# Attention, top-1 MoE and soft MoE in one kernel: seven weight chunks are issued ahead of four others

## The chip, the cores and the metric

One NeuronCore of a Trainium2 chip runs the whole program. The metric is the device time of one execution in microseconds (us); lower is better. All inputs and outputs are float32.

## What is computed

Three layers follow each other: causal attention with a cumulative bias, a mixture of experts that sends each token to one of 8 experts, and a soft mixture of experts with 32 slots. The work around the change is the end of the second layer and the whole of the third.

```python
# x: 2304 tokens x 512 from the attention
for e in range(8):                                # layer 2: one expert per token
    xe = x[expert_idx == e]
    out[expert_idx == e] = gate_w[...] * (np.maximum(xe @ w1[e], 0) @ w2[e])
# layer 3: soft MoE, phi: 512 x 32
logits = x @ phi
d = softmax(logits, axis=0)                       # over tokens
slot_input = (d.T @ x).reshape(8, 4, 512)
for e in range(8):
    slot_out[e] = np.maximum(slot_input[e] @ w1[e], 0) @ w2[e]
c = softmax(logits, axis=1)                       # over the 32 slots
return c @ slot_out.reshape(32, 512)
```

## The kernel before, in words

**Stages.** The attention runs first. From 241.6 us of the span on, layer 2 goes through the experts one by one: `step_unit` (line 1020 multiplies) makes the hidden rows, and the eight functions of `post_units` fold the expert's tokens into the 32 slot inputs `SI`. The last of them, `p4` (line 1160), multiplies with the four `w2` chunks of the expert. For the last expert there is no later expert beside which this could run, so its `post` functions stand alone, in the loop at line 1318, with filler products (`warm`) on TensorE between them. Layer 3 comes last: `f1` (line 1386) multiplies the slot inputs with 32 chunks, `f3` (line 1425) the hidden rows with 32 more, in three blocks of output columns (`COLS`: 256, 128 and 128 wide), and `finish` makes and writes the output of a block (lines 1456 to 1458).

**Chunks and slots.** All weights of layers 2 and 3 come in chunks of 128 partitions x 1024 float32 (512 KB), numbered in the order in which they are used. `M1` is 96: chunks 0 to 95 belong to layer 2 (`ORD`), 96 to 159 to layer 3. The last four of layer 2, 92 to 95, are the `w2` chunks of the last expert. Of layer 3, 96 to 127 are `m1` (used by `f1`), 128 to 143 `m2` and 144 to 159 `m3` (used by `f3`). A chunk gets its place in SBUF from `slot`, which counts the places handed out: a ring of `RING` = 34 slots in three pools (`NFIFO`), so that chunk i + 34 goes where chunk i was. When layer 2's products are done, seven more places appear: the tile `x3`, where the transposed tokens `xT` were (three chunks), and the pool `fifo_d`, where the pool `weights` (split weights and gathered tokens) was (`NLATE` = 4 chunks). `slot` has a number, `first`, from which on the seven are handed out; after these the ring goes on.

**What sets the order.** `fill(n)` issues the DMA of every chunk up to n - 1 that has not been issued, in order of number, on the SP queue. `refill(i)` stands behind the last use of chunk i and lets `fill` go as far as the slot of i allows. Instructions of an engine run in program order, and so does the SP queue: a DMA that waits for its slot holds back every DMA behind it. Line 1317 issues the seven extra chunks. Chunk 126 is the one that takes the slot of chunk 92, the first `w2` chunk of the last expert, and `fill` counts straight on, so all of 126 to 136 are asked for at line 1317, ahead of `post` in the program text. The output is written by DMAs of the SP queue too (line 1458), behind the last chunk. In layer 3, five slots of the ring serve other tiles (`extra`, positions in `EXTRA`), among them the three `c` tiles, which POOL loads from DRAM (line 1349) after its scatters into it (line 1187).

Of the kernel before, what the change touches and what calls it, by code (L numbers as in the profile page):

```python
# [38 lines left out]
NLATE = 4  # L39
RING = sum(NFIFO)  # L40
# [9 lines left out]
M1 = len(ORD)  # L50
# [5 lines left out]
EXTRA = {2: 0, 3: 2, 4: 3, 5: 4, 8: 1}  # L56
# [25 lines left out]
def kernel(ctx, tc, qk, vm, vt, s, wg, w1, w2, phi, m1, m2, m3, out, dbg=None):  # L82
# [52 lines left out]
    def chunk_src(i):  # L135
        if i < M1:
            kind, e, c = ORD[i]
            w, c = (w1 if kind == "w1" else w2), c + 4 * (kind == "wt")
            return w[bass.ds(place[e], 1), c].rearrange("o p n -> (o p) n") if e else w[0, c]
        i -= M1  # L140
        if i < 32:
            return m1[i // 8 * 2 + i % 2, i % 8 // 2]
        if i < 48:
            return m2[(i - 32) // 2, i % 2]
        return m3[(i - 48) // 8, i % 8]

    slot_n = [0]

    def slot(shape, dtype, name):

        i, first = slot_n[0], M1 + RING
        slot_n[0] += 1
        if first <= i < first + 3:
            return x3[0][:, i - first]
        if i >= first + 3:
            k = (i - first - 3) % (NLATE + RING)
            if k < NLATE:
                return fifo[3].tile(shape, dtype, tag="c3", name=name)
            i = k - NLATE + first

        a, b, c = NFIFO
        r = (i - a - b) % RING
        k = int(i >= a) if i < a + b else 0 if r < a else 2 if r < a + c else 1
        return fifo[k].tile(shape, dtype, tag=f"c{k}", name=name)

    def fill(upto, eng=None):
        while len(chunk_t) < min(upto, M1 + 64):
            i = len(chunk_t)
            chunk_t[i] = slot([128, 1024], F32, f"chunk{i}")
            (eng or nc.sync).dma_start(out=chunk_t[i], in_=chunk_src(i))  # L170
# [5 lines left out]
    def refill(i):  # L176
        if i == 0 or len(fifo) < 3 or not place or not full:
            return
        fill(i + 1 + RING + (NLATE + 3 - sum(x <= i - M1 for x in EXTRA) if i >= M1 else 0))

# [706 lines left out]
    def prep(n, ov=False, lo_later=None):  # L889
        if n >= E * 8 or (n in wh_t and not ov):  # L890
            return
        e, j = divmod(n, 8)
        i = CID["w1", e, j // 2]
        raw = half(i, j % 2, ov)
        hi, lo = (wpool[0].tile([128, 512], F32R, tag="xg" if ov else "w" + t, name=f"w{t}{n}", bufs=3)
                  for t in ("hi", "lo"))
        nc.scalar.copy(hi, raw)  # L897
        def low(eng):
            eng.tensor_tensor(out=lo, in0=raw, in1=hi.bitcast(F32), op=ALU.subtract)  # L899

        if lo_later is None:
            low(nc.vector)
        else:
            lo_later.append(low)
        wh_t[-1 if ov else n] = (hi, lo)
        if not ov and j % 2:
            refill(i)
# [145 lines left out]
    def p_unit(e, ov=False):  # L1053
        def f():
            pt = ps.tile([128, 256], F32, tag="y1", name=f"pt{e}", bufs=1)
            for k in range(4):
                i = CID["wt", e, k]
                w = [half(i, h, ov) for h in range(2)]
                for g in range(4):
                    nc.tensor.matmul(pt[32 * g:32 * g + 32, :], lhsT=phi_sb[:, k, :], rhs=w[g // 2][:, 256 * (g % 2):256 * (g % 2) + 256],  # L1060
                                     start=(k == 0), stop=(k == 3), skip_group_check=True)
                if not ov:
                    refill(i)
            P_t[0] = mp.tile([128, 256], F32, tag="P", name=f"P{e}", bufs=1)
            nc.vector.transpose(P_t[0], pt)
        return f
# [23 lines left out]
    def post_units(e, idx, final=False, ov=False):  # L1090
# [64 lines left out]
        def p4():  # L1155
            al, G = d["al"], d["G"]
            si = ps.tile([128, DM], F32, tag="y2", name=f"si{e}", bufs=1)
            for j in range(8):
                g = 32 * (j % 4)
                nc.tensor.matmul(si[g:g + 32, :], lhsT=G[:, 32 * j:32 * j + 32], rhs=half(CID["w2", e, j // 2], j % 2, ov),  # L1160
                                 start=(j < 4), stop=(j >= 4), skip_group_check=True)
                if j % 2 and not ov:
                    refill(CID["w2", e, j // 2])
            for x in (slice(0, 256), slice(256, 512)) if final else (slice(0, 512),):
                nc.vector.scalar_tensor_tensor(out=SI[:, x], in0=SI[:, x], scalar=al[:, 0:1], in1=si[:, x],
                                               op0=ALU.mult, op1=ALU.add)
# [89 lines left out]
    with tc.manual_schedule():  # L1256
# [57 lines left out]
        late.close()  # L1314
        lp = ctx.enter_context(tc.tile_pool(name="fifo_d", bufs=NLATE))
        fifo.append(lp)
        fill(M1 + RING + 3 + NLATE)
        for i, x in enumerate(("p1", "p2", "pg0", "pg1", "pg2", "p4", "p4b", "pc", "pc2")):
            post[x]()
            if i in WARM:  # L1320
# [2 lines left out]
        for j in range(2):  # L1323
            sps = ps.tile([128, 2, 32], F32, tag="tp", name=f"sps{j}", bufs=2)
            for k in range(2):
                x = 256 * j + 128 * k
# [12 lines left out]
        def extra(i):  # L1339

            if i < 2:
                hz_t[i] = slot([128, 4, 8, 32], F32, f"hz{i}")
                nc.gpsimd.memset(hz_t[i], 0.0)
            else:
                t = slot([128, 960], F32, f"c{i}")
                c = t[:, 0:768].rearrange("p (t r s) -> p t r s", t=6, r=4)
                cl = t[:, 768:960]
                for x, d in zip((cl, t[:, 0:192], t[:, 192:384]), c_d):
                    nc.gpsimd.dma_start(out=x, in_=d.rearrange("(p t) s -> p (t s)", t=18)[:, 192 * i - 384:192 * i - 192])
                c_t[i - 2] = c, cl, t  # L1350
# [185 lines left out]
```

## Time and profile before

| | us |
|---|---|
| device time, median of 3 runs | 512.91 (512.44 to 514.46) |
| device time of the profiled execution | 517.06 |
| its span, from first to last instruction | 515.2 |
| TensorE busy | 477.4 (93%) |
| TensorE weight loads busy | 337.6 (66%) |
| VectorE busy | 313.7 (61%) |
| ScalarE busy | 250.6 (49%) |
| GpSimd busy | 183.7 (36%) |
| DMA queue of SP, share of 16 engines | 67.0% |

The profiled execution is one run of its own, 4.15 us above the median; 1.86 us of its time lie outside the span. All times below count from the start of its span. The shares are means over stages with different limits: layer 3 begins at 454.7 us and is about a ninth of the span. Matmuls are pipelined, so a busy TensorE need not be at its peak.

### The profile page before, as it was taken

How to read it: one execution, taken by the hardware profiler on the slowest of the kernel's cores; microseconds unless marked ns; L12 is line 12 of the kernel's file. 1: busy time of each engine (PE TensorE's matmuls, PEld its weight loads, DVE VectorE, ACT ScalarE, POOL GpSimd, SP SyncE). 2: the span in 40 equal slices, each digit the busy share in tenths (PEclk: the TensorE clock that was granted, in tenths of full speed). 3: DMA queues.
4: the chain of work that ended last, by engine and by line, in shares of the span. 5: the costliest groups of instructions: out<-in, count | busy, mean ns of one | idle time of the engine just before them, and what ended most of it. 6: DMA issues, size and time to landing. Idle time of an engine off the chain costs nothing.

```text
span 515.2 us, 11829 instructions
## 1 busy us (share of the span) xinstructions
PE 477.4 (93%) x4313; PEld 337.6 (66%) x4318; DVE 313.7 (61%) x910; ACT 250.6 (49%) x700; POOL 183.7 (36%) x248
## 2 busy tenths in 40 slices
PE   7888899999999999998979999999999999999876
PEld 2466666677677676677858777777777777434445
DVE  6586768977897798454743746565657566222322
ACT  4466877767767776741323434344344434111202
POOL 6234430953294335160143333333324031236000
PEclk9789999999999999999998999999999999999985
DMA  3755665376646542313699999994996967599998
GB/s 113 257 174 178 197 217 180 80 244 203 213 140 221 184 145 93 112 40 101 239 384 405 408 405 408 406 337 125 396 405 209 377 236 295 202 352 391 408 401 278
DMA packets 45171, 130.87 MB, mean 254 GB/s; under 512 B 6191, under 2 KB 14705, under 8 KB 43184
## 3 DMA queue, kind: packets, MB, share of 16 engines
q1 hardware_dynamic: 42016, 123.34, 67.0%
q0 software_dynamic: 2896, 6.66, 3.8%
q8 instruction: 36, 0.59, 0.5%
q14 instruction: 31, 0.25, 0.1%
q10 hardware_dynamic: 192, 0.01, 0.0%
HBM read 114.78 MB, written 11.13 MB: 244 GB/s over the span
## 4 chain that ended last, share of the span: by engine, by line
PE 35%; DMA 9%; DVE 3%; issue 2%; ACT 2%; POOL 0%; POOLq 0%; DVEq 0%; SPq 0%; ACTq 0%
PE h L1020 17%; DMA chunk<-in_m_dram 7%; PE gt L1140 3%; PE pt L1060 2%; PE si L1160 2%; PE op L1456 2%; PE xTp L1011 2%; DMA xg<-xg_d,sidxu 1%; PE lg L1077 1%; DMA chunk<-in_w_dram 1%; PE hp L1386 1%; PE gt L1150 1%; PE acc L1425 1%; PE warm L249 1%; PE lr L1107 1%
## 5 line engine op out<-in xcount | busy, mean ns | idle before, releaser
L1020 PE MATMUL h<-xT,whi 128*128 128x304 f32 (+5 forms) x512 | 114.2, 314 | 1.5 <-ACTq L1197 1.5
L1020 PEld LDWEIGHTS h<-xT,whi 128*128 128x128 f32 x512 | 84.1, 190 | 15.6 <-issue 11.7
L1020 PE MATMUL h<-xT,wlo 128*128 128x256 f32 (+5 forms) x256 | 77.6, 303 | 0.0
L494 ACT COPY aT<-tp 128x512 f32<-128x512 f32 (+3 forms) x128 | 55.4, 452 | 43.4 <-PE tp L487 31.1
L428 DVE CUSTOM_DVE_ANT_0 sa<-sc,mask 128x384 f32<-128x384 f32 (+3 forms) x128 | 60.6, 484 | 23.9 <-PE sc L425 21.7
L438 ACT ACTIVATE sa<-sa,mx 128x128 f32<-128x128 f32 (+3 forms) x128 | 71.2, 561 | 2.1 <-DVE mx L428 1.7
L1048 ACT ACTIVATE hb<-h 128x304 f32<-128x304 f32 (+5 forms) x64 | 26.9, 420 | 73.6 <-PE h L1020 61.5
L541 PE MATMUL oTp<-aT,v 128*64 128x320 f32 (+4 forms) x448 | 59.5, 374 | 0.0
L487 PE MATMUL tp<-ident,sa 128*128 128x128 f32 x320 | 53.8, 285 | 2.2 <-ACT sa L438 2.1
L899 DVE TENSOR_TENSOR wlo<-chunk,whi 128x512 fp32r<-128x512 f32 x61 | 41.7, 683 | 22.6 <-ACT whi L897 22.2
L425 PE MATMUL sc<-ks,qs 128*128 128x384 f32 (+3 forms) x128 | 51.7, 406 | 2.8 <-DVE mx L428 2.5
L390 POOL TENSOR_TENSOR ks<-qk,ks 64x576 fp32r<-64x576 f32 x31 | 45.4, 1479 | 16.1 <-ACT ks L370 12.2
L425 PE MATMUL sc<-kb,qs 128*128 128x384 f32 (+3 forms) x128 | 42.6, 332 | 7.3 <-DMA kb<-trs 2.8
L487 PEld LDWEIGHTS tp<-ident,sa 128*128 128x128 f32 x320 | 35.4, 143 | 21.1 <-issue 11.4
L1187 POOL DMA_INDIRECT c_d<-L,idxm x22 | 22.9, 1041 | 73.4 <-DVE wlo L899 59.0
L1020 PEld LDWEIGHTS h<-xT,wlo 128*128 128x128 f32 x256 | 48.6, 190 | 0.0
L370 POOL CAST ks<-qk 128x1152 fp32r<-128x1152 f32 x13 | 14.9, 1149 | 72.8 <-PE sc L452 67.7
L897 ACT CAST whi<-chunk 128x512 fp32r<-128x512 f32 x64 | 39.0, 612 | 0.2 <-DVE ch L712 0.2
L541 PEld LDWEIGHTS oTp<-aT,v 128*64 128x64 f32 (+1 forms) x448 | 24.0, 135 | 20.1 <-issue 14.3
L1085 DVE STREAM_TRANSPOSE hk<-hb 128x320 f32<-128x320 f32 (+3 forms) x64 | 29.6, 480 | 5.4 <-PE gu L1140 4.5
L425 PEld LDWEIGHTS sc<-kb,qs 128*128 128x128 f32 x128 | 25.3, 198 | 8.6 <-DVE qs L376 3.0
L425 PEld LDWEIGHTS sc<-ks,qs 128*128 128x128 f32 x128 | 25.4, 199 | 7.9 <-DVE mx L428 4.0
(279 smaller groups left out, 847.7 us busy)
## 6 DMA issues: line engine op xcount, KB each, us to landing
chunk<-in_w_dram SPq DMA_DIRECT2D x96, 512.0 KB
chunk<-in_m_dram SPq DMA_DIRECT2D x61, 512.0 KB
qk<-in_qk_dram SPq DMA_DIRECT2D x15, 1152.0 KB
kb<-ks SPq DMA_DIRECT2D x15, 288.0 KB
v<-in_vm_dram SPq DMA_DIRECT2D x16, 256.0 KB
xg_d<-xr SPq DMA_DIRECT2D x16, 256.0 KB
out_dram<-ob SPq DMA_DIRECT2D x4, 512.0 KB
out_dram<-ob SPq DMA_DIRECT2D x5, 384.0 KB
```

What stands on the lines that cost most here:

```text
L390: eng.tensor_tensor(out=ks, in0=qk_t[p][64:128, 1, hh], in1=ks.bitcast(F32), op=ALU.subtract)
L425: nc.tensor.matmul(sc[:, :ext], lhsT=qs_t[p % 2][:, j, hh, 64 * hh + 128 * st:64 * hh + 128 * st + 128], rhs=ks[:, hh, :ext], start=(j == ...
L428: nc.vector.tensor_tensor_reduce(out=sa[:, o:o + ext], in0=sc[:, :ext], in1=mask[:, 512 - ext:512], scale=1.0, scalar=3.0e38, op0=ALU.add, ...
L438: nc.scalar.activation(out=x, in_=x, func=ACTF.Exp, bias=mx[:, st:st + 1], scale=-1.0, accum_out=rsum[:, b, st, 2 * k + hh:2 * k + hh + 1])
L487: nc.tensor.transpose(tp[:, 128 * c:128 * c + 128], src(hh, st, jt), ident)
L494: nc.scalar.copy(o, i)
L541: nc.tensor.matmul(o[c][64 * hh:64 * hh + 64, lo - 256 * c:hi - 256 * c], lhsT=v_t[p][:n, jt, hh, :], rhs=aT[:n, hh, jt, lo:hi], start=(jt ...
L897: nc.scalar.copy(hi, raw)
L899: eng.tensor_tensor(out=lo, in0=raw, in1=hi.bitcast(F32), op=ALU.subtract)
L1020: nc.tensor.matmul(out[:, :w_], lhsT=a, rhs=b[:, :w_], start=first, stop=last, skip_group_check=True)
L1048: nc.scalar.activation(out=hb[:, (8 * e + j) % 5, :w_], in_=h[:, :w_], func=ACTF.Relu)
L1085: nc.vector.transpose(hkv[:, j, 0:w_], hb[:, (8 * e + j) % 5, 0:w_])
```

## The change

The seven places are handed out four chunks earlier: `first` is 126 where it was 130. Chunks 126 to 128 go into `x3`, 129 to 132 into `fifo_d`, and 133 to 136 take the `w2` slots of the last expert. `refill` counts the extra places from chunk 92 on, so that 133 to 136 are issued behind `p4`'s uses of 92 to 95, and line 1317 issues up to chunk 132. Size, source and number of the DMAs stay as they were, and so does the code of every engine but SP's order.

```diff
@@ slot
-        i, first = slot_n[0], M1 + RING
+        i, first = slot_n[0], M1 + RING - 4
@@ refill
-        fill(i + 1 + RING + (NLATE + 3 - sum(x <= i - M1 for x in EXTRA) if i >= M1 else 0))
+        fill(i + 1 + RING + (NLATE + 3 - sum(x <= i - M1 for x in EXTRA) if i >= M1 - 4 else 0))
@@ end of the expert loop
         late.close()
         lp = ctx.enter_context(tc.tile_pool(name="fifo_d", bufs=NLATE))
         fifo.append(lp)
-        fill(M1 + RING + 3 + NLATE)
+        fill(M1 + RING - 1 + NLATE)
```

On the SP queue, at the end of layer 2, this is the order before, with the semaphores for which each DMA waits. Chunk 126 is named by its number, and the three DMAs into `x3` are chunks 130 to 132. DMAHW0 to 7 are semaphores that SP's DMAs take in turn, so each waits for the landing of the DMA eight places ahead of it; DMASW0 to 7 are those of GpSimd's DMAs; PE_49 is TensorE's.

```order
L170 DMA chunk125_9345<-in_m1_dram 128x1024 [waits DMAHW6_49,PE_49]
L170 DMA chunk126_9360<-in_m1_dram 128x1024 [waits DMAHW7_49,PE_49]
L170 DMA chunk127_9362<-in_m1_dram 128x1024 [waits DMAHW0_49,PE_49]
L170 DMA chunk128_9364<-in_m2_dram 128x1024 [waits DMAHW1_49,PE_49]
L170 DMA chunk129_9366<-in_m2_dram 128x1024 [waits DMAHW2_49,PE_49]
L170 DMA x3_9355<-in_m2_dram 128x1024 [waits DMAHW3_49]
L170 DMA x3_9355<-in_m2_dram 128x1024 [waits DMAHW4_49]
L170 DMA x3_9355<-in_m2_dram 128x1024 [waits DMAHW5_49]
L170 DMA chunk133_9371<-in_m2_dram 128x1024 [waits DMASW5_49,DMASW4_49,DMASW6_49,DMASW3_49,DMASW7_49,DMASW2_49,DMAHW6_49,DMASW1_49,DMASW0_49]
L170 DMA chunk134_9373<-in_m2_dram 128x1024 [waits DMAHW7_49]
L170 DMA chunk135_9375<-in_m2_dram 128x1024 [waits DMAHW0_49]
L170 DMA chunk136_9377<-in_m2_dram 128x1024 [waits DMAHW1_49]
```

Here the four DMAs that wait for TensorE (126 to 129) stand ahead of the seven that don't. The same place in the changed kernel, where the DMAs into `x3` are chunks 126 to 128:

```order
L170 DMA chunk125_9345<-in_m1_dram 128x1024 [waits DMAHW6_49,PE_49]
L170 DMA x3_9355<-in_m1_dram 128x1024 [waits DMAHW7_49]
L170 DMA x3_9355<-in_m1_dram 128x1024 [waits DMAHW0_49]
L170 DMA x3_9355<-in_m2_dram 128x1024 [waits DMAHW1_49]
L170 DMA chunk129_9363<-in_m2_dram 128x1024 [waits DMASW5_49,DMASW4_49,DMASW6_49,DMASW3_49,DMASW7_49,DMASW2_49,DMAHW2_49,DMASW1_49,DMASW0_49]
L170 DMA chunk130_9365<-in_m2_dram 128x1024 [waits DMAHW3_49]
L170 DMA chunk131_9367<-in_m2_dram 128x1024 [waits DMAHW4_49]
L170 DMA chunk132_9369<-in_m2_dram 128x1024 [waits DMAHW5_49]
L170 DMA chunk133_9457<-in_m2_dram 128x1024 [waits DMAHW6_49,PE_49]
L170 DMA chunk134_9461<-in_m2_dram 128x1024 [waits DMAHW7_49,PE_49]
L170 DMA chunk135_9465<-in_m2_dram 128x1024 [waits DMAHW0_49,PE_49]
L170 DMA chunk136_9469<-in_m2_dram 128x1024 [waits DMAHW1_49,PE_49]
```

The seven moved ahead as one piece, and the wait for GpSimd's DMAs moved with the first DMA into `fifo_d`. From chunk 137 on the rows are the same in both.

## Rows read from the trace of the kernel before

**Rows 1.** The page: span, and its 40 slices of 12.9 us (granted clock, DMA)
```profile
span 515.2 us, 11829 instructions
...
PEclk9789999999999999999998999999999999999985
DMA  3755665376646542313699999994996967599998
GB/s 113 257 174 178 197 217 180 80 244 203 213 140 221 184 145 93 112 40 101 239 384 405 408 405 408 406 337 125 396 405 209 377 236 295 202 352 391 408 401 278
```

**Rows 2.** Chain that ended last, in order of time (start, us, what), from 459 us
```profile
459.86 14.45 DMA chunk<-in_m_dram
...
489.69 10.14 DMA chunk<-in_m_dram
...
499.88 1.08 PE acc L1425 x16
500.95 1.47 PE op L1456 x6
...
505.45 5.03 PE op L1456 x24
510.50 0.48 ACT ob L1457
```

**Rows 3.** Busy time by stretch, then granted clock, DMA share, GB/s
```profile
446.50:454.00 7.50, 7.29 (x98) 3.16 (x83) 2.13 (x8) 0.63 (x2) 0.00 (x0) 1.00 0.30 108
447.50:451.50 4.00, 3.94 (x45) 1.00 (x30) 0.45 (x1) 0.37 (x1) 0.00 (x0) 1.00 0.00 0
454.00:500.00 46.00, 40.43 (x540) 19.36 (x544) 12.20 (x38) 7.00 (x14) 12.41 (x19) 0.99 1.03 401
500.00:506.00 6.00, 6.00 (x51) 5.05 (x51) 1.89 (x5) 0.96 (x2) 0.00 (x0) 0.50 1.09 378
506.00:508.00 2.00, 2.00 (x11) 2.00 (x11) 1.34 (x3) 0.54 (x2) 0.00 (x0) 0.50 0.89 275
508.00:513.00 5.00, 2.46 (x12) 2.27 (x11) 1.12 (x2) 1.37 (x3) 0.00 (x0) 0.50 1.02 297
```

**Rows 4.** Waits of the SP queue, 441 to 456 us (total, times, longest)
```profile
SPq L170 <- PE si L1160: 9.2, 1, 9.2
```

**Rows 5.** Timeline of the SP queue, single issues (start, us)
```profile
441.37 0.38 SPq L170 DMA_DIRECT2D chunk<-in_m_dram  x1
451.01 0.33 SPq L170 DMA_DIRECT2D chunk<-in_m_dram  x1
454.65 0.33 SPq L170 DMA_DIRECT2D chunk<-in_m_dram  x1
478.19 0.33 SPq L170 DMA_DIRECT2D chunk<-in_m_dram  x1
511.00 0.51 SPq L1458 DMA_DIRECT2D out_dram<-ob  x1
```

**Rows 6.** Timeline of TensorE and its weight loads, single groups (PEld: weight load)
```profile
438.91 1.92 PE L1160 MATMUL si<-chunk,G 128*32 128x512 f32 x16
449.92 1.92 PE L1160 MATMUL si<-chunk,G 128*32 128x512 f32 x16
478.17 0.18 PEld L1425 LDWEIGHTS acc<-chunk,hz 128*32 128x32 f32 x8 [0.25 <-DMA chunk<-in_m_dram]
492.24 0.65 PE L1425 MATMUL acc<-chunk,hz 128*32 128x128 f32 x16 [0.20 <-DMA chunk<-in_m_dram]
```

**Rows 7.** Waits, 436 us to the end (total, times, longest)
```profile
PE acc L1425 <- DMA chunk<-in_m_dram: 4.7, 10, 0.6
```

**Rows 8.** Busy time by stretch, as rows 3, in the last third of layer 3
```profile
478.00:490.00 12.00, 10.41 (x166) 6.16 (x162) 5.00 (x11) 2.90 (x7) 0.00 (x0) 1.00 1.03 409
490.00:493.00 3.00, 2.68 (x54) 1.68 (x42) 1.87 (x4) 1.00 (x2) 0.00 (x0) 1.00 1.02 408
493.00:496.00 3.00, 1.29 (x32) 0.75 (x32) 0.00 (x0) 0.00 (x0) 0.00 (x0) 1.00 1.02 403
498.50:501.00 2.50, 2.06 (x33) 1.18 (x33) 0.00 (x0) 0.00 (x0) 0.00 (x0) 0.57 1.04 381
```

**Rows 9.** Timeline of GpSimd: scatters into c_d, and loads from it
```profile
438.14 0.98 POOL L1187 DMA_INDIRECT c_d<-L,idxm  x1 [0.30 <-issue]
...
455.29 1.05 POOL L1187 DMA_INDIRECT c_d<-L,idxm  x1 [10.10 <-DVE inv L1332]
...
462.92 4.38 POOL L1349 DMA_DIRECT2D c<-c_d  x8 [1.12 <-DMA c_d<-L,idxm]
```

## The prediction, made before the changed kernel ran

> **What bounds the kernel now.** The page comes first, for the shape of the run. Its DMA row is mixed for the first half; at the end it stands at 9 in almost every slice, with about 400 GB/s, and just ahead of that end lies one slice of 209 GB/s [rows 1]. The chain that ended last says what this means for the end: from 459.86 us it runs through DMAs of chunks (pieces of 14.45 and 10.14 us among them), and TensorE takes it over for good only at 499.88 us, when the last chunks have come [rows 2]. So layer 3 is paced by the loading of its weights, not by its arithmetic, though the page gives TensorE 93% of the whole span.
>
> The stretches then give the pace of the load and the hole ahead of it. From 454 to 500 us the DMA engines are full (share 1.03, 401 GB/s), and they stay full to 506 (1.09). The last writes are slower in bytes but full in time: 1.02 at 297 GB/s from 508 to 513 [rows 3]. From 447.5 to 451.5 they move nothing at all. The whole hole is seen in the stretch 446.5 to 454.0: share 0.30 of 7.5 us, so 0.70 x 7.5 = 5.25 us of standing still [rows 3]. TensorE has no use for chunks in that time: it is busy with the last expert's products and with filler. But the load that later bounds it could have run.
>
> The SP queue tells why the engines stand still. It issues chunk 125 at 441.37 us and the next, 126, only at 451.01 [rows 5]. The longest wait there is one of 9.2 us for `si`, line 1160, the product that uses up the last expert's `w2` chunks [rows 4]; that product begins at 449.92 [rows 6]. Behind 126 stand seven DMAs whose places were free long before: the last product that reads `xT` and the split weights of `weights` ends just ahead of the previous expert's `si`, which begins at 438.91 [rows 6].
>
> **The change, step by step.** Nothing is added or removed: 64 chunks of 512 KB, as before, on the same queue. Eleven DMAs change places.
>
> *The seven that go ahead (126 to 132).* In the new order none of them waits for TensorE, only for the landing of the DMA eight places ahead of it. SP is free at 441.37 + 0.38 = 441.75 us [rows 5]; at some 0.45 us an issue the three into `x3` and chunk 129 are out by about 443.5, and 130 to 132 follow as 122 to 124 land. The engines are still carrying 122 to 125 until about 447. The price of one chunk comes from two arrivals that TensorE waited for: 141 at 478.17 and 152 at 492.24 [rows 6], so 14.07 / 11 = 1.28 us. Seven chunks are 9.0 us of work, against 5.25 us of hole: the hole is filled from 447 to the point where the old stream began, and 3.7 us of the seven remain.
>
> *The four that go behind (133 to 136).* They go out when the first product over `w2` has run, at 451.01 us as 126 did. By then the engines have work until 447 + 9.0 = 456, so their wait of 9.2 us now costs nothing; the margin is 5 us. Who is queued behind the waiting DMA: chunk 137 and all that follow. 137 needs the slot of chunk 96, which `f1` uses from 454.7 on, as before, so it isn't made later either.
>
> *The wait for GpSimd's DMAs*, at the first DMA into `fifo_d`, moves from 454.65 us [rows 5] to about 443. What it can wait for is the scatter that began at 438.14 [rows 9], and by 447.5 nothing moves on any DMA queue [rows 3], so it has landed. At worst chunk 129 goes out at 447.5, when the three into `x3` still hold 3.8 us of work. Cost 0.
>
> *The traffic beside the last expert's work.* From 447 to 452 the reads now run beside `post`. Bounds: the same `si` product takes 1.92 us at 438.91, with DMAs around it, and 1.92 at 449.92 with none [rows 6], which gives 0. For the other end I allow the 0.5 us by which TensorE is late without being waited for, below. I take 0.
>
> *Sum at the DMA engines.* The stream behind the hole starts 5.25 us earlier, stays full, and moves the same bytes, so the last write ends 5.25 us earlier. I call it 5.3, since the stretch 506 to 508 has another 0.11 x 2 = 0.2 us of slack [rows 3] of which a part may go too. At no point can more than the hole be won: 5.5 us with that slack is the upper end.
>
> *Does TensorE follow?* It waits for chunks 4.7 us in all in layer 3 [rows 7], ten waits between 478.17 and 500 us. Chunks that come 5.3 us earlier leave it none of these but the last ones. So TensorE's own work ends at least 4.7 us earlier, and after it the order is as now: last copy of `ob` at 510.98 [rows 2], last write issued at 511.00 [rows 5], when the engines still have about 2 us of earlier writes to move. A lone last write of 192 KB then ends with the rest. Lower end 4.7, upper 5.5, and I take 5.3, because the engines are full at the end and they set it.
>
> A rule bears on this step. In the trace, DMA standing still from 447.5 to 451.5 lies beside a TensorE busy 3.94 of 4 us [rows 3]. The Trainium skill, Perfetto Trace Analysis, section Optimization Strategies, says to work on the engines that the matmul engine waits for while it is idle; by it, the hole beside a busy TensorE would be worth nothing by itself, and only the waits for chunks would count. The sum would be 4.7 by the one and 5.3 by the other.
>
> **Result.** Against its own execution: 517.06 - 5.3 = 511.8 us, span 509.9. The median of the runs shown is 4.15 us below that execution; the work of layer 3 is the same in both, so I take the same 5.3 from it: 512.91 - 5.3 = **507.6 us**.
>
> **Rivals.**
>
> *The clock gives part of it back.* TensorE's granted clock is 1.00 to 498.5 us, then 0.57 and 0.50 [rows 8], that is, 2.4 and then 1.2 GHz; before it fell, TensorE had been busy 1.29 of 3 us (493 to 496), waiting for chunks. If in the changed kernel it fell as early as the start of the third column block, the rest would run at the low level: eight groups at 1.08 us, 36 output products at (1.47 x 2 + 5.03) / 36 = 0.22, two sums of about 0.5 and the last copy of 0.48 [rows 2], 18.1 us. The block begins at 492.24 now [rows 6], less the 1.9 us that TensorE stands idle from 478 to 493 [rows 8]: 490.3. It would end at 508.4 instead of 510.98, a gain of 2.5: 510.4 us. Against it: fewer waits leave TensorE busier than it is now when the clock is still full. The Trainium skill, TensorE: Matmul & The Clock Gate, section HAM oscillation, tells of kernels whose clock falls when products wait for DMAs; by that rule, too, shorter waits speak for a clock that stays up. If it does, the products end earlier still, and the writes set the end: no more than the 5.5 above.
>
> *The seven don't go early.* Some wait that the rows don't show keeps them to 451 us; then the hole stays: 512.9. For it: the order shows which semaphores are waited for, not their values. Against it: `x3` waits for SP's own DMAs alone.
>
> *Slower.* The wait for GpSimd's DMAs at chunk 129 now stands ahead of eight DMAs that the end needs, at 443 us. Were it to include the last expert's two scatters, the first of which begins at 455.29, it would last until GpSimd's loads from the scattered table start, 462.92 [rows 9]. The engines would have the three chunks of `x3` and then nothing; the stream would restart at 462.9, not at 452, with three chunks fewer: 10.9 - 3.8 = 7 us lost, 519.9 us. It decides as soon as the wait lasts past 447 + 3.8 + 5.3 = 456. Against it: the same wait was over at 454.65 [rows 5], ahead of these scatters.
>
> **How the numbers follow.** Forecast (gain of 4.7 to 5.5, with the spread of the runs some 506.0 to 509.0): 0.76. Clock: 0.10. Not early: 0.10. Slower: 0.04. The range goes from 506.0 (5.5 and 1.4 us of spread between medians; the three runs shown span 2.0) to 510.8, which takes in the clock rival, and leaves out not early and slower. A measurement of this kernel tells about 0.5% from no change, 2.6 us, so faster means under 510.35: the forecast and half of the clock rival, 0.81; same: the other half and not early, 0.15; slower 0.04.
>
> **What would show it.** Right: SP issues 126 at about 441.8 us and 132 before 447.5; no stretch of 1 us without DMA between 442 and the end; 133 still at about 451; TensorE's waits for chunks in layer 3 far below 4.7 us, and none before 490; the last write some 5 us earlier; layers 1 and 2 unmoved. Wrong: a hole that comes back after 456, `post` longer than now (the first product of `f1` later than 454.7), a clock that falls before 495, or a DMA rate after 447 below 400 GB/s.

## The result, and the profile after

| | before | changed |
|---|---|---|
| median device time, us | 513.68 (512.44 to 514.98, 4 runs) | 508.10 (506.58 to 510.09, 4 runs) |
| ratio to before, 95% interval | | 0.9894 (0.9862 to 0.9927) |
| device time of the profiled execution | 517.06 | 506.58 |
| its span | 515.2 | 504.8 |
| start of the last expert's `w2` product (`si`) | 449.92 | 445.15 |
| from there to the end of the span | 65.28 | 59.65 |

The change is 5.6 us faster by the medians. The two spans differ by 10.4 us, but 4.8 of these arise ahead of the change, where both kernels have the same program: the `si` product starts that much earlier. So absolute times of the two profiles must not be compared; the stretch from `si` to the end can be, and it is 5.63 us shorter. The products that it is counted from, in the changed kernel (start, us): `si`, and the first of layer 3.

```profile
445.15 1.92 PE L1160 MATMUL si<-chunk,G 128*32 128x512 f32 x16
449.95 7.07 PE L1386 MATMUL hp<-chunk,sT 128*32 128x512 f32 x64 [0.87 <-DVE sT L1328]
```

The page of the changed kernel (span; DMA share and GB/s in 40 slices, here of 12.6 us):

```profile
span 504.8 us, 11829 instructions
...
DMA  3866655276647543313399999994996977899998
GB/s 107 267 185 179 222 200 187 62 266 206 216 122 224 190 152 105 121 41 101 134 395 405 406 406 408 406 406 156 359 407 246 358 246 287 310 411 395 403 398 274
```

The slice of 202 GB/s near the end of before's row [rows 1] is gone: 310, 411, 395, 403, 398. Busy time by stretch (columns as in rows 3) shows it closer; the first stretch lies around `si` as 446.5 to 454.0 did before:

```profile
441.73:449.23 7.50, 7.29 (x98) 3.17 (x83) 2.12 (x8) 0.63 (x2) 0.00 (x0) 1.00 1.03 412
449.23:479.00 29.77, 28.96 (x339) 12.45 (x340) 7.02 (x29) 4.19 (x9) 12.55 (x19) 1.00 1.03 401
479.00:489.00 10.00, 9.67 (x199) 7.11 (x198) 4.95 (x10) 2.83 (x5) 0.00 (x0) 1.00 1.02 402
489.00:495.00 6.00, 5.44 (x65) 4.70 (x66) 3.46 (x8) 1.92 (x4) 0.00 (x0) 1.00 1.08 380
495.00:498.00 3.00, 0.74 (x7) 0.59 (x6) 0.88 (x2) 0.96 (x2) 0.00 (x0) 1.00 1.13 347
498.00:502.00 4.00, 0.00 (x0) 0.00 (x0) 0.00 (x0) 0.00 (x0) 0.00 (x0) 0.67 1.08 310
502.00:503.00 1.00, 0.00 (x0) 0.00 (x0) 0.00 (x0) 0.00 (x0) 0.00 (x0) 0.50 0.33 99
```

The share was 0.30 [rows 3] and is 1.03 (a full stretch reads a little over 1 in these profiles); from there the engines are full until 502 us, and the last writes end within a microsecond or so of that. TensorE, VectorE, ScalarE and GpSimd are busy for the same times in the first stretch as before, to 0.01 us: the reads beside the last expert's work cost it nothing.

The SP queue (start, us) shows the new order:

```profile
437.04 0.47 SPq L170 DMA_DIRECT2D x<-in_m_dram  x1
...
439.04 0.33 SPq L170 DMA_DIRECT2D chunk<-in_m_dram  x1
...
441.77 0.33 SPq L170 DMA_DIRECT2D chunk<-in_m_dram  x1
...
446.24 0.33 SPq L170 DMA_DIRECT2D chunk<-in_m_dram  x1
```

These are chunk 126, the first into `x3`; 129, the first into `fifo_d`; 132, the last of the seven; and 133, the first into a `w2` slot. 126 follows 125 at once, where it came 9.64 us behind it before [rows 5]. The wait for `si` is still there, at 133, but costs the engines nothing; it is 3.2 us now, where it was 9.2 [rows 4]:

```profile
SPq L170 <- PE si L1160: 3.2, 1, 3.2
```

TensorE's waits for chunks in layer 3 fell from ten and 4.7 us [rows 7] to one, which ends at 489.55 us; below it the end of the chain that ended last (start, us, what):

```profile
PE acc L1425 <- DMA chunk<-in_m_dram: 0.9, 1, 0.9
```

```profile
479.10 10.41 DMA chunk<-in_m_dram
...
489.55 0.65 PE acc L1425 x16
...
492.97 2.78 PE op L1456 x21
...
495.77 0.48 ACT ob L1457
```

The last copy of `ob` ends at 496.25, 51.1 us behind the start of `si`; before it was 61.06. So TensorE's part became 10 us shorter, not 5.6, since the clock stayed at its full level to the last product (1.00 to 498 us, against 0.57 and 0.50 from 498.5 on before [rows 8, rows 3]). The other 4.3 us are worth nothing: the engines are full of writes until 502 us, and a third busy in the microsecond behind it.

### The profile page after: what moved, and what is told of

It is laid out like the page before. It is cut to its first block, busy times and chain, and to the rows that moved or that the text cites. A ratio compares the mean times of both kernels' runs of the same rounds, so it can differ in the third digit from the quotient of the medians.

```text
span 504.8 us, 11829 instructions
## 1 busy us (share of the span) xinstructions
PE 470.2 (93%) x4313; PEld 332.7 (66%) x4318; DVE 312.6 (62%) x910; ACT 250.5 (50%) x700; POOL 184.6 (37%) x248
## 4 chain that ended last, share of the span: by engine, by line
PE 39%; DMA 5%; DVE 3%; issue 2%; ACT 2%; POOL 0%; SPq 0%; DVEq 0%; POOLq 0%; ACTq 0%
PE h L1020 17%; PE gt L1140 4%; PE si L1160 3%; PE hp L1386 3%; PE pt L1060 2%; DMA chunk<-in_m_dram 2%; PE xTp L1011 2%; PE acc L1425 2%; PE lg L1077 1%; DMA xg<-xg_d,sidxu 1%; DMA chunk<-in_w_dram 1%; PE op L1456 1%; PE gt L1150 1%; PE lr L1107 1%; PE warm L249 1%
## 5 line engine op out<-in xcount | busy, mean ns | idle before, releaser
L1020 PEld LDWEIGHTS h<-xT,whi 128*128 128x128 f32 x512 | 83.9, 190 | 15.5 <-issue 11.7
L541 PE MATMUL oTp<-aT,v 128*64 128x320 f32 (+4 forms) x448 | 59.5, 374 | 0.0
```

Of the source, the lines that this page charges most:

```text
L541: nc.tensor.matmul(o[c][64 * hh:64 * hh + 64, lo - 256 * c:hi - 256 * c], lhsT=v_t[p][:n, jt, hh, :], rhs=aT[:n, hh, jt, lo:hi], start=(jt ...
L1020: nc.tensor.matmul(out[:, :w_], lhsT=a, rhs=b[:, :w_], start=first, stop=last, skip_group_check=True)
```

## The experiments

All times "from `si`" are the span's end less the start of the last expert's `w2` product in the profile of that run: 65.28 before, 59.65 with the change.

### Three of the seven go ahead

The edit is against the changed kernel.

```diff
-        if i >= first + 3:
-            k = (i - first - 3) % (NLATE + RING)
+        if first + 3 <= i < first + 7:
+            i -= 3
+        elif i >= first + 7:
+            k = (i - first - 7) % (NLATE + RING)
             if k < NLATE:
                 return fifo[3].tile(shape, dtype, tag="c3", name=name)
-            i = k - NLATE + first
+            i = k - NLATE + first + 4
...
-        fill(M1 + RING - 1 + NLATE)
+        fill(M1 + RING + 3 + NLATE)
```

> Only the three chunks that go into x3 are moved ahead of the four that wait for the last expert's w2 slots; the four for fifo_d stay behind these. Theory (the load of layer 3 is one stream, and the hole of 5.25 us in it is what the change fills): three chunks fill 3 x 1.28 = 3.8 us of the hole, about 1.4 us of it stays open, and the time falls by 3.8 us against before (ratio about 0.9925), two thirds of what the whole change gives. Rival 1 (what matters is that the SP queue is not blocked at all, or that TensorE's clock stays up): the same as the whole change, 5.5 us. Rival 2 (the four in fifo_d are what matters): less than 1 us. In the profile the stretch from the first product over the last expert's w2 to the end is 65.3 us before and 59.6 with the change; the theory wants about 61.5 here.

Measured: 511.22 us, ratio 0.9937 (0.9913 to 0.9960). From `si` 448.49 to 510.4: 61.9 us, a gain of 3.4. The stretch around `si`:

```profile
445.07:452.57 7.50, 7.36 (x99) 3.18 (x83) 2.12 (x8) 0.63 (x2) 0.00 (x0) 1.00 0.83 308
```

104 GB/s short of the changed kernel's 412 over 7.5 us is 1.9 us of load left undone, against 5.5 before (108 GB/s). The gain follows the part of the hole that is filled: 3.6 of 5.5 us, and 3.4 at the end. Neither "all" nor "none" fits.

### The clock kept up, the hole left

```diff
             for u in merge(units, side):
                 u()
+                if h == 2 and u in units:
+                    warm(3, "y3")
```

> The kernel before, with three filler products of 512 columns behind each of the eight chunks of the third column block, so that TensorE stays busy there and its clock should not fall to the low level at 498.5 us. The hole in the loads stays. Theory (the DMA engines set the end): a gain of at most 0.5 us, although TensorE's last products run up to twice as fast. Rival (the change wins by the clock that it keeps up): a gain of 3 us or more, and with the clock kept up a stretch from the last expert's w2 product to the end of 62 us or less instead of 65.3.

Measured: 514.15 us, ratio 0.9996 (0.9977 to 1.0016). From `si`, 446.96, to 512.2: 65.2 us, as before. Busy time by stretch, and the last copy:

```profile
498.50:501.00 2.50, 2.50 (x30) 1.82 (x29) 0.85 (x2) 0.48 (x1) 0.00 (x0) 1.00 1.09 381
501.00:506.00 5.00, 3.94 (x32) 3.53 (x31) 3.50 (x7) 2.40 (x5) 0.00 (x0) 1.00 1.08 343
506.00:510.00 4.00, 0.00 (x0) 0.00 (x0) 0.00 (x0) 0.00 (x0) 0.00 (x0) 0.68 1.06 306
```

```profile
504.99 0.48 ACT ob L1457
```

The clock is 1.00 to 506 us, and the last copy ends 58.5 us behind `si` instead of 61.1: some 2.5 us earlier. The end doesn't move, since the DMA engines are full with writes until 510 us (1.06 from 506 on). Within what the interval can tell (about 1 us), the clock of the last products is worth nothing here.

### The same order on SP, with before's places

```diff
+        for i in range(M1 + RING - 4, M1 + RING):
+            chunk_t[i] = slot([128, 1024], F32, f"chunk{i}")
         fill(M1 + RING + 3 + NLATE)
...
             post[x]()
+            if x == "p4":
+                for n in range(M1 + RING - 4, M1 + RING):
+                    nc.scalar.dma_start(out=chunk_t[n], in_=chunk_src(n))
```

> The kernel before, with its own assignment of chunks to places (126 to 129 go into the w2 slots), but these four are issued on ScalarE's queue behind the product that frees the slots, so they hold back nobody on the SP queue. Theory (order on the queue is all that matters, which chunk sits where is not): the seven go out at about 441.8 us, and the gain is that of the change, 5.3 us (ratio about 0.99). Rival (the chunks 126 to 129 are needed first and it is their early arrival that counts): no gain, since they still come last of the eleven. Cost to allow for: four issues of 0.4 us on ScalarE ahead of its exponential for the last scatter, up to 1 us on the way to the scatters.

Measured: 508.99 us, ratio 0.9900 (0.9871 to 0.9928). From `si`, 447.02, to 506.6: 59.6 us. The stretch around `si`, and ScalarE's queue:

```profile
443.60:451.10 7.50, 7.35 (x99) 3.18 (x83) 2.12 (x8) 0.63 (x2) 0.00 (x0) 1.00 1.02 411
```

```profile
448.12 1.89 ACTq L1324 DMA_DIRECT2D chunk<-in_m_dram  x4
```

The four wait on another queue for the same product, and the whole gain is there. So it is the order of the waits on SP's queue that cost the time; which chunk lies where doesn't matter, nor that 126 to 129 come before 130 to 136 in use, since `f1` begins with its last eight chunks, 120 to 127, no sooner than 15.5 us after the first of the four is issued (448.12):

```profile
463.58 3.64 PE L1391 MATMUL hp<-chunk,sT 128*32 128x512 f32 x32
```

### Two loads fewer

```diff
+            if i >= M1 + 62:
+                chunk_t[i] = chunk_t[M1 + 61]
+                continue
             chunk_t[i] = slot([128, 1024], F32, f"chunk{i}")
```

> The changed kernel without the loads of the last two chunks, 158 and 159: the last two groups of products in the third column block read chunk 157 in their place, so 1 MB less is moved and the products are as many. Theory (with the hole filled the DMA engines are still what sets the end): 2 x 1.28 = 2.6 us less than the changed kernel, 8.1 less than before (ratio about 0.984). Rival (the change has made TensorE or the copies the bound): no more than 0.5 us less than the changed kernel (ratio 0.989).

Measured: 507.73 us, ratio 0.9849 (0.9817 to 0.9882). From `si`, 450.05, to 506.9: 56.85 us, 2.8 less than the change; 2.6 was expected, so the loads still set the end of the changed kernel. But TensorE is not far behind: with the two loads gone it is never idle from 485 to 495 us, where the changed kernel still had its one wait of 0.9 us.

```profile
485.00:490.00 5.00, 5.00 (x82) 3.48 (x81) 2.54 (x4) 2.24 (x4) 0.00 (x0) 1.00 1.02 404
490.00:495.00 5.00, 5.00 (x137) 4.35 (x136) 2.15 (x5) 0.32 (x1) 0.00 (x0) 1.00 1.07 381
```

The medians alone would not have told it: this one is 6.8 us below its own runs of before, the change in its three timings 5.6, 7.4 and 6.9. In this run's profile `si` began at 450.05, 4.9 us later than in the changed kernel's, in a program that is the same up to there.

### The change again, and two attempts to go further

The changed kernel was timed twice more, beside the next kernels.

> The changed kernel again, on the chip and beside the runs of before that the next three kernels have, so that these can be set against it. All theories: ratio 0.989, between 0.986 and 0.992. In its profile the stretch from the last expert's w2 product to the end is 59.6 us (65.3 before).

Measured: 507.86 us, ratio 0.9860 (0.9829 to 0.9890), from `si` 59.8 us.

*An earlier `w2` product* moves `p4` of the last expert but one:

```diff
-                         lg_unit(e, 0), q["pc2"], s_[5], t_[4], s_[6], t_[5]]
+                         lg_unit(e, 0), q["pc2"], s_[5], t_[4], *([q["p4"]] if e + 1 == E else []), s_[6], t_[5]]
...
-                units = [s_[7], t_[6], q["p4"], lg_unit(e, 1), t_[7], post["pl"]]
+                units = [s_[7], t_[6], lg_unit(e, 1), t_[7], post["pl"]]
```

> The changed kernel with one step moved: the w2 product of the last expert but one (p4, line 1160) comes ahead of the hidden rows of step 6 of the last expert, some 3 to 4 us earlier, so that the four chunks 122 to 125, which take its slots, are issued earlier. Between 434 and 442 us the loads have gaps too (share 0.71 over 7 us before). Theory (with the stream unbroken to the end, every microsecond of a gap ahead of it that is filled is won): of the some 2 us of gap 1.5 to 2 us go, ratio about 0.986. Rival (the gaps ahead of 442 cost nothing, since the change's own seven chunks could not start earlier anyway): same as the change. In the profile the stretch from that last w2 product to the end falls to about 58 us.

Measured: 508.23 us, ratio 0.9863 (0.9825 to 0.9902), from `si` 57.2 us: no difference from the change that the times show, though the stretch is 2.6 us shorter than in the change beside it. It was run a second time, with the change beside it.

> The kernel with the earlier w2 product again, beside the changed kernel in the same call, because its first timing did not tell it from the change (508.23 and 507.86 us) though its profile was 2.6 us shorter from the first product of layer 3 to the end (52.4 and 55.0). Theory: the gain at the end is real and some 0.5 us of it is given back, since TensorE now has nothing to do between the last hidden rows and the sums that need them: 1.5 to 2 us less than the change. Rival: what is won at the end is lost in full ahead of layer 3 (first product of layer 3 some 2 us later, counted from the first product of layer 2): no difference.

> The changed kernel once more, as the one beside which the earlier w2 product is set. All theories: ratio between 0.986 and 0.992 against before, 59.6 to 59.8 us from the last expert's w2 product to the end, 55.0 us from the first product of layer 3 to the end.

Measured: 507.16 us, ratio 0.9847 (0.9810 to 0.9884), and 507.59 for the change, 0.9853 (0.9811 to 0.9894), just under the 0.986 that was expected. The first product of layer 3, in the first run of this kernel:

```profile
452.56 5.79 PE L1386 MATMUL hp<-chunk,sT 128*32 128x512 f32 x52 [0.87 <-DVE sT L1328]
```

From it to the end of the span of 505.0 are 52.4 us, and 52.2 in the second run, against 55.0 and 54.7 in the two runs of the change beside them: 2.5 us are won there in both. In the stretch that ends 8 us ahead of the last `si` the share rose from 0.73 to 0.88, so most of the gap was filled (the change first, then the first run of this kernel):

```profile
433.40:440.40 7.00, 6.34 (x59) 4.53 (x57) 3.72 (x12) 1.42 (x4) 3.17 (x3) 1.00 0.73 234
432.76:439.76 7.00, 6.66 (x54) 4.03 (x52) 3.42 (x10) 1.42 (x4) 3.17 (x3) 1.00 0.88 335
```

But the medians differ by +0.4 and -0.4 us, with intervals of about 0.35% on each side. From the first product of layer 2 to the first of layer 3 it took 212.6 and 212.0 us against 211.6 and 211.8, so 0.2 to 1.0 us are given back there. What becomes of the rest isn't settled; that this version is faster than the change is not shown.

*Two column blocks instead of three*, so that the second half of the output is written in runs of 1 KB:

```diff
-        COLS = ((0, 256), (256, 128), (384, 128))
+        COLS = ((0, 256), (256, 256))
...
-            nt, parts = ((2, (4, 4, 4, 4, 2)), (3, (6, 6, 6)), (3, (3, 6, 6, 3)))[h]
+            nt, parts = 2, (4, 4, 4, 4, 2)
```

(with the layout of `m3` and the loops over the blocks to match)

> The changed kernel with two blocks of 256 output columns instead of 256, 128 and 128: as many bytes, but the last half of the output is written in runs of 1 KB instead of 512 bytes. In the changed kernel the engines are full to the end with loads at 410 GB/s, then the first writes at about 385 and the last at 300 to 320. Theory (the DMA engines set the end): 2.4 MB at 385 instead of some 310 GB/s, 1.5 us less than the change, ratio about 0.986. Rival (with one block fewer, all output products and copies of the last half come after the last chunk, and these set the end): 1 us or more slower than the change.

Measured: 511.54 us, ratio 0.9939 (0.9905 to 0.9974), slower than the change. From `si` 60.5 us, 0.7 to 1.0 more than in the three profiles of the change. Busy time by stretch (the third row is the changed kernel, in the profile of the result, as far behind `si` as the first), and the chain:

```profile
498.00:502.00 4.00, 2.80 (x15) 2.48 (x14) 2.67 (x5) 1.17 (x2) 0.00 (x0) 0.75 0.50 175
502.00:506.00 4.00, 1.36 (x7) 1.06 (x5) 1.77 (x3) 1.17 (x2) 0.00 (x0) 0.82 1.03 339
493.05:497.05 4.00, 2.69 (x21) 2.41 (x21) 2.60 (x6) 1.92 (x4) 0.00 (x0) 1.00 1.12 361
```

```profile
499.55 3.83 PE op L1456 x18
```

The engines have written the first half and then wait for the second: a share of 0.50, where the changed kernel has 1.12. All 18 output products of the last block come behind the last chunk, which is the rival's reason. It explains 0.7 to 1.0 us; the median is 3.7 above the change's, and where the other 2.8 or so come from stays open (`si` began late in this profile, at 450.10).

*Both edits:*

> Both edits together. Theory: they act on the same stream at its two ends, so the gains add: some 3 us less than the change, ratio about 0.983. Rival: one hides the other, no better than the better one alone.

Measured: 509.47 us, ratio 0.9892 (0.9860 to 0.9924). From `si` 59.0 us. Not better than the change alone.

## Why the prediction was right, point by point

**The sum.** 5.3 us were forecast at the DMA engines and 5.63 measured from `si` to the end. The step was right and its size a little low. The working set the share of 0.30 against 1; a full stretch of this kernel reads 1.03. By bytes the hole is (412 - 108) / 412 x 7.5 = 5.5 us, and with the slack of 0.2 us at 506 to 508, which went too, 5.7. The upper end named was 5.5. The changed kernel has some slack of its own in its last microsecond (share 0.33 from 502 to 503 us), so the terms are known to about half a microsecond, not better.

**The medians.** That they gave 5.6 us too, and 508.10 against a forecast of 507.6, is in part luck. The two repeats gave 7.4 and 6.9, while the stretch from `si` in their profiles was 59.8 and 59.5 us, as in the first. The three intervals have 5.7 to 7.1 us in common, which begins above the 5.5 named as the most that can be won. What the repeats show beyond the hole stays open; no profile of before was taken beside them.

**Seven ahead, four behind.** Chunk 126 goes out 0.43 us behind 125, and 133 at 1.1 us behind the start of `si`, as 126 did before. Between, the share is 1.03. The margin for the four held.

**The wait for GpSimd's DMAs.** Chunk 129 went out at 439.04 us, 2.0 us behind 126, while the engines had 126 to 128 to carry: cost 0, as said. The slower rival falls with it.

**Traffic beside the last expert's work: 0.** Confirmed to 0.01 us of busy time, and the first product of `f1` begins 4.80 us behind `si` in both kernels.

**TensorE or the loads.** The waits of TensorE were 4.7 us, the hole 5.5; the gain is 5.63. The run with three chunks ahead, and the one with two loads fewer, show that the end follows the bytes. The rule of the Trainium skill that was weighed there (Perfetto Trace Analysis, Optimization Strategies) gives 4.7, as it was read there; the measurement decides for the hole, since the stretch was 59.5 to 59.8 us in the three profiles of the change, and 65.2 to 65.3 in the two with the whole hole. Here, engines that stood still beside a busy TensorE were worth their full time, because a later stage was bound by them.

**The clock.** The rival was that it falls earlier; it fell later, only when TensorE had finished. As forecast, the writes then set the end. That the level of the clock in the last products doesn't move the end was argued in the prediction and is shown, within about 1 us, by the run that held it.

**What did not hold.** Layers 1 and 2 were expected to stay unmoved. Their program is the same, but from one profile to the next the first product of layer 3 began anywhere from 449.95 to 454.9 us; why isn't known. The signs that were named in absolute times have to be shifted by the 4.8 us between the two profiles: the one wait left, ending at 489.55, would be at 494.3 in the profile before, behind the 490 that was named. The forecast of 507.6 took no harm from it, since it was made from the stretch and not from absolute times. One number of the page was misread too: the slice with the hole is the one of 202 GB/s [rows 1], not that of 209, which lies at about 390 us; no term hung on it.

## What to carry to other kernels

Where a late stage is paced by loads, look for the last stretch ahead of it in which the DMA engines stand still, and ask which DMA at the head of the queue waits, for whom, and which DMAs behind it wait for nothing. The gain to expect is the hole, in bytes not moved, up to what the DMAs behind can fill, and not what the compute engine is seen to wait, as long as that engine can follow. Compare stretches between the same two events in both profiles before spans are compared.

## What the runs showed that was not expected

The time from the start of the span to the last expert's `w2` product varied from 445.15 to 448.40 us over the three profiles of the changed kernel, and up to 450.10 in kernels that are the same up to there. A change of 2 us in layer 3 is therefore plain in a stretch of the profile and can be missed by medians of four to ten runs.

The output's last writes, in runs of 512 bytes, go at 297 to 310 GB/s with the engines full (shares 1.02 [rows 3] and 1.08); the same half of the output in runs of 1 KB went at 339 GB/s with a share of 1.03, and not at the 385 on which that expectation was built.
